# Gated mix of memory attention and a SiLU network on one core: q, k, v from scaled fp16 halves instead of float32r halves

## The chip, the cores and the metric

The kernel runs on one core of a Trainium2 chip. The metric is the device time of one execution in microseconds (us), from the kernel's start to its end. A core has TensorE (PE; its weight loads are listed as PEld), VectorE (DVE), ScalarE (ACT), GpSimd (POOL) and SyncE (SP), which here issues every DMA.

## The reference

x has 2048 rows of 448 features, 16 heads of 28 and 4 segments of 512 rows. Attention inside a segment adds the mask written below; between segments a linear memory carries over.

```python
q, k, v = x @ wq, x @ wk, x @ wv              # (16 heads, 4 segments, 512, 28)
phi = lambda t: jnp.where(t > 0, t + 1.0, jnp.exp(t))
g = sigmoid(beta)                              # one number a head
for s in range(4):
    mask = (ar[:, None] < ar[None, :]) * (-1e9)
    a_dot = softmax(qs @ ks.T * Dh ** -0.5 + mask) @ vs
    a_mem = (phi(qs) @ M) / (phi(qs) @ z + 1e-6)
    o = g * a_mem + (1.0 - g) * a_dot
    M, z = M + phi(ks).T @ vs, z + phi(ks).sum(rows)
a = o @ wo
b = silu(x @ w1) @ w2                          # 448 -> 1792 -> 448
gate = sigmoid((x * gate_w).sum(-1))
out = gate * a + (1 - gate) * b
```

## The kernel before, in words

Every float32 operand is kept as two halves, a high and a low part, and a product takes eleven matmuls: for each of three chunks of 128 features high·high, low·high and high·low, and two for the last 64 features, whose low part of x lies in the free half of the partitions (`passes`, line 368). `product` (L555) issues them and is also used by the feed-forward network and by the output projection, so L563 is the matmul line of all three.

There are two sorts of halves. For q, k, v before the change, `xquarter` (segment 0) and `xfeat` (segments 1 to 3) copy x into an xT tile as float32r (ACT, L779 and L795) and subtract to get the low part (DVE L783, L784; POOL L800, L802). `weight` does the same for wq, wk, wv (ACT L819, the subtraction at L822 on DVE or POOL). For the network, `halves` (L520) multiplies by a power of two first and stores fp16: ACT L523 for the high part, then `rest` (L512) for the low part, one DVE instruction (L515) or two POOL ones (L517, L518). `x16` (L531) loads x a second time, into rawf, and makes the fp16 tile xh of a segment with it; segment 0 during the projections, segments 1 to 3 inside the network.

The powers of two come from sizes. `size` (L380) reduces a tile to the largest absolute value of each partition (DVE L387). `scales(a, b)` (L398) turns columns a to b of these into scales: a reduction (L413), a transpose on PE (L417), four small DVE steps (L420 to L424), a broadcast on PE (L426), and two DVE steps that write the scale `up` and its inverse `top` (L430, L431). Index 0 to 3 is x of a segment, then WV, WQ, HQ (sixteen columns of w1 ride along in each block of wq and wk; HQ and HK scale their products), WK, HK, W1, W2, WO.

`project` (L699) is the first stage. For each block t of four heads in a segment (16 blocks) `proj` (L844) makes q and k in an "mm" bank of PSUM, evicts a high and a low fp16 half (ACT L853, DVE L855, both scaled by a column of `sqk`) and sends them to DRAM; where the memory needs it, it also makes phi: `pr` = relu(−t) from PSUM (ACT L869), `pe` = exp(−pr) (ACT L871), `ph` = max(t, 0) + pe (DVE L872). `vproj` (L892) makes v of 128 rows in an "sc" bank with the gate as a 449th column, and evicts it likewise (ACT L903, DVE L907, scaled by `sv`; ACT L905 takes the gate's exponential). `memory` and `retrieve` update and read the memory. `maxima` and `attention` are the masked attention, in the second stage, over which the network's matmuls are spread: `unit` (L1086) takes one segment's first matrix (L563 into mm), the SiLU (ACT L1098, DVE L1100, ACT L1102, DVE L1104), and the second matrix (L1121). The exponentials of attention are ACT L1224, the high half of their result ACT L1236, its low half POOL L1240, the product with v PE L1253. The last stage adds attention's output through wo.

The order on each engine is written when the program is built: `Sched` (L115) is a list scheduler. Tasks have an engine (or a choice of DVE and POOL: `either`, and `scaled` for two-pass work), a duration from a formula, dependencies, buffers that they take, and a priority; at each step the task that can start first goes next, and among equals the one of lower priority number. So the numbers at the head of the file (VC, QS, KS1, SS, OT1, XS, FIRST, WOT and others) move tasks against each other on every engine, and the engines then run that order strictly. Fifteen warm-up matmuls (L743) run at the very start.

Of the kernel before, what the change touches and what calls it, by code (L numbers as in the profile page):

```python
# [19 lines left out]
NG = 4  # L20
# [10 lines left out]
NEG = -1.0e30  # L31
NT = NSEG * NG
# [13 lines left out]
WOT = 59.67  # L46
# [8 lines left out]
SLACK = 0.88  # L55
LOP = 11.21
LATE = 0.08
FIRST = 120.0
WPRIO = 120.0
MAXO = 66.73  # L60
# [3 lines left out]
MP = 13.22  # L64
VF = 2.5
VA = 1.36
VS = 11.08
NV = 8
XS0 = 1.75
VC = -7.68  # L70
OT1 = 8.22
XS = 6.38
QS = -4.77
KS1 = 0.43
SS = 5.62
# [6 lines left out]
PRICE = 34.19  # L82
PVRUNS = [((1, 0), 1)]
PVP = 44.58
FLO = -16.6
FHI = 688.88
WOP = 89.36
SZ = 27.69
SZSTEP = 2.77
XPRIO = 87.67  # L90
WBP = -20.36
# [152 lines left out]
def infini_mix(ctx: ExitStack, tc: tile.TileContext, x, wq, wk, wv, wo, beta, w1, w2, out):  # L244
# [90 lines left out]
    WV, WQ, HQ, WK, HK, W1, W2, WO, NS = range(NSEG, NSEG + 9)  # L335
    cols, at = {}, 0
    for j, n in enumerate([4] * (NSEG + 5) + [FREE, FB, 4]):
        cols[j] = (at, at + n)
        at += n
# [11 lines left out]
    own2 = const.tile([128, 2], F32, name="own2")  # L351
    upw = const.tile([128, 3], F32, name="upw")
    sqk = const.tile([128, 2 * NSEG], F32, name="sqk")
# [4 lines left out]
    sv = const.tile([128, NSEG], F32, name="sv")  # L358
# [7 lines left out]
    X16 = {0: base.tile([128, 7, L], F16, name="xh0")}  # L366
# [11 lines left out]
    SIZE, SCALED, XH = {}, {}, {}  # L378
# [58 lines left out]
    LATER, GDONE, QREADY, KREADY, END1 = [], [], {}, {}, []  # L437

    def xi(s):
        return slice(NSEG - 1 - s, NSEG - s)  # L440

    def weigh(j, prio, *deps):

        def go():
            c = (j - WQ) // 2
            nc.vector.tensor_scalar(upw[:, 2:3], up[:, j:j + 1], own2[:, 0:1], None, op0=OP.mult)
            nc.vector.scalar_tensor_tensor(upw[:, c:c + 1], up[:, j + 1:j + 2], own2[:, 1:2], upw[:, 2:3], op0=OP.mult,
                                           op1=OP.add)
        return dve(350, go, SCALED[j], *deps, prio=prio)

    VREADY, PREADY, EREADY, OREADY = {}, {}, {}, {}

    def vscale(s, prio, *deps):
        VREADY[s] = dve(130, lambda: nc.vector.tensor_scalar(sv[:, s:s + 1], up[:, WV:WV + 1], up[:, xi(s)], 2.0 ** -26,
                                                             op0=OP.mult, op1=OP.mult), SCALED[NSEG - 1 - s], *deps, prio=prio)

    def qscale(s, prio, *deps):
        QREADY[s] = dve(130, lambda: nc.vector.tensor_scalar(sqk[:, s:s + 1], upw[:, 0:1], up[:, xi(s)], 2.0 ** -26,
                                                             op0=OP.mult, op1=OP.mult), SCALED[NSEG - 1 - s], *deps, prio=prio)

    def kscale(s, prio, *deps):

        def go():
            nc.vector.tensor_scalar(sqk[:, NSEG + s:NSEG + s + 1], upw[:, 1:2], up[:, xi(s)], 2.0 ** -26, op0=OP.mult,
                                    op1=OP.mult)
            if s < NSEG - 1:
                nc.vector.tensor_scalar(spk[:, s:s + 1], up[:, WK:WK + 1], up[:, xi(s)], 2.0 ** -25, op0=OP.mult, op1=OP.mult)
                nc.vector.tensor_scalar(spk[:, s:s + 1], spk[:, s:s + 1], UP, None, op0=OP.min)
        KREADY[s] = dve(400, go, QREADY[s], *deps, prio=prio)

    def others(s, prio, bds, own, t_own, t_gh):
# [13 lines left out]
        PREADY[s] = pool(600, spread_out, dve(260, go, VREADY[s], KREADY[s], prio=prio), t_own, t_gh, prio=prio)  # L485
# [45 lines left out]
    def x16(s, prio, *deps):  # L531

        ALL, END = slice(None), slice(REM, 128)
        XH[s] = []
        deps = [derive(s, SCALED[NSEG - 1 - s], prio), *deps]
        for c in range(4):
            r = Buf(RAW)
            d = dma(262e3, lambda c=c, r=r: start(r.v, x[s, :, c]), *deps, takes=[r], prio=prio + 0.01 * c)
            if s == 0:
                sl = slice(c * 128, (c + 1) * 128)  # L540
                hi = (ALL, slice(0, 4), sl)
                lo = [((ALL, slice(4, 7), sl), (ALL, slice(0, 3)), (ALL, slice(0, 3), sl)),
                      ((END, NC, sl), (END, NC), (END, NC, sl))]

                def src(r=r):
                    return r.v.rearrange("p (c n) -> p c n", c=4)
            else:
                hi = (ALL, c)
                lo = [((ALL, 4 + c), (ALL,), (ALL, c)) if c < NC else ((END, NC), (END,), (END, NC))]

                def src(r=r):
                    return r.v
            XH[s] += halves(NSEG - 1 - s, hi, lo, lambda: X16[s], src, L, d, prio + 0.01 * c, uses=[r])
# [37 lines left out]
    WA, WB = {}, {}  # L591
# [44 lines left out]
    XT, XDONE = {}, {}  # L636
# [62 lines left out]
    def project():  # L699
        es = ExitStack()  # L700
        wp = es.enter_context(tc.tile_pool(name="pw", bufs=1))
        XTR = cycle([wp.tile([128, 7, L], F32R, name=f"xT{i}") for i in range(2)])
        W = {n: wp.tile([128, 8, D + 2 if n == "v" else L], F32R, name=f"w{n}s") for n in "qkv"}
# [11 lines left out]
        ring("xraw", [128, L], F32, 6)  # L715
# [17 lines left out]
        def c1():  # L733
            for v in vtiles:
# [15 lines left out]
        LATER.append(dve(300, lambda: (nc.vector.tensor_reduce(own2[:, 0:1], ident[:, :GW], axis=AX.X, op=OP.max),  # L750
                                       nc.vector.tensor_reduce(own2[:, 1:2], ident[:, GW:], axis=AX.X, op=OP.max)), t_id, prio=-40))
# [8 lines left out]
        XR = {}  # L760

        def load_x(s, c, prio, *deps):
            b = Buf(R["xraw"])
            d = dma(262e3 if s else 170e3, lambda: start(b.v, x[s, :, c]), *deps, takes=[b], prio=prio)
            XR[s, c] = b, d
            if s:
                size(NSEG - 1 - s, lambda: b.v, L, d, uses=[b], prio=prio + XS)

        def xquarter(tb, prio):
            b, d = XR.pop((0, tb))  # L770
            if tb == 0:
                XT[0] = Buf(XTR)
                XDONE[0] = []
            xt = XT[0]
            sl = slice(tb * 128, (tb + 1) * 128)

            def view():
                return b.v.rearrange("p (c n) -> p c n", c=4)
            hi = act(L + 45, lambda: nc.scalar.activation(xt.v[:, 0:4, sl], view(), AF.Copy), d, *XDONE[0][:1],  # L779
                     takes=[] if tb else [xt], uses=[b, xt], prio=prio)  # L780

            def lo():
                nc.vector.tensor_sub(xt.v[:, 4:7, sl], view()[:, 0:3], raw(xt.v[:, 0:3, sl]))  # L783
                nc.vector.tensor_sub(xt.v[REM:128, NC, sl], view()[REM:128, NC], raw(xt.v[REM:128, NC, sl]))  # L784
            XC[0, tb] = [hi, dve(L + 64, lo, hi, uses=[b, xt], prio=prio)]
            XDONE[0] += XC[0, tb]
            size(NSEG - 1, lambda: b.v, L, XC[0, tb][1], uses=[b], prio=prio + XS0)

        def xfeat(s, c, prio):
            b, d = XR.pop((s, c))  # L790
            if c == 0:
                XT[s] = Buf(XTR)
                XDONE[s] = []
# [615 lines left out]
```

## Time and profile before

| what | value |
|---|---|
| median of the runs | 558.04 us (557.48 to 558.3, 3 runs) |
| span of the profiled execution, first to last instruction | 555.5 us |
| mean granted clock of TensorE | 0.997 |
| matmul records | 4007 |
| DMA moved | 85.87 MB, of which 52.60 MB read from and 26.09 MB written to HBM |
| last float32r matmul of q, k, v starts | 153.3 us |
| attention's last matmul with v starts | 466.6 us |

The profile gives the execution's span and no other time of its own; the runs lie 2.5 us above the span at the median, for what comes ahead of the first instruction and behind the last.

In a row of the groups or of the timeline stand the source line, the engine, the operation, the tile written and those read, the shapes and the count; in the groups behind a bar the busy time in us, the mean of one in ns, and the idle time of the engine just before them with what ended it. In the table by stage each engine has its busy time and its number of instructions. The chain of waits is followed back from the last instruction.

### The profile page before, as it was taken

To read this page: it belongs to the slowest core of one execution; us is meant where nothing else is said; L and a number is where in the kernel's file an instruction comes from. 1 tells how busy PE (TensorE), PEld (TensorE's weight loads), DVE (VectorE), ACT (ScalarE), POOL (GpSimd) and SP (SyncE) were. 2 spreads that over 40 slices of the span, in tenths; PEclk is the share of its full clock that TensorE was granted. 3 is DMA by queue.
4 is the path that set the end of the run, shared out by engine and by line. 5 is a ranking of instruction groups with operands and counts; after the bars stand their busy time and mean duration, and the time that the engine had idled before them with its cause. 6 is when DMAs were issued, how large, how long until landed. Compare 5 with 4: busy or idle time off the path is not lost.

```text
span 555.5 us, 11580 instructions
## 1 busy us (share of the span) xinstructions
PE 541.9 (98%) x4007; PEld 340.2 (61%) x4007; DVE 413.6 (74%) x1076; ACT 399.7 (72%) x695; POOL 365.2 (66%) x520
## 2 busy tenths in 40 slices
PE   8799999999999999999999999999999999999997
PEld 5588888888844555555656545565556555555544
DVE  6997998788789966789656888857997228745463
ACT  6467988876656878899778978878998897403140
POOL 5813648637320777999899979998999996212220
PEclk9899999999999999999999999999999999999999
DMA  8479888986775445423344235357302213689972
GB/s 293 153 241 217 229 220 242 224 213 188 216 211 163 130 136 176 122 74 79 108 118 127 68 88 155 108 139 180 90 19 70 69 50 94 226 208 222 251 183 83
DMA packets 91497, 85.87 MB, mean 155 GB/s; under 512 B 55432, under 2 KB 79112, under 8 KB 91440
## 3 DMA queue, kind: packets, MB, share of 16 engines
q1 hardware_dynamic: 91440, 85.15, 55.6%
q8 instruction: 31, 0.51, 0.4%
q14 instruction: 26, 0.21, 0.1%
HBM read 52.60 MB, written 26.09 MB: 142 GB/s over the span
## 4 chain that ended last, share of the span: by engine, by line
PE 84%; POOL 5%; DVE 4%; ACT 3%; DMA 2%; issue 2%; DVEq 0%; POOLq 0%; ACTq 0%
PE mm L563 32%; PE mm L1121 22%; PE sc L563 11%; PE sc L668 5%; PE sc L1219 5%; PE cc L1253 5%; POOL phl L1240 3%; DMA rawf<-in_x_dram 1%; ACT pf L1224 1%; PE cc L973 1%; ACT phl L1236 1%; DVE sizes L387 1%; PE cc L936 1%; DMA xraw<-in_x_dram 1%; PE cc L974 1%
## 5 line engine op out<-in xcount | busy, mean ns | idle before, releaser
L1240 POOL TENSOR_TENSOR phl<-pf,phl 128x384 f16<-128x384 f32 (+1 forms) x192 | 189.2, 1004 | 14.9 <-ACT phl L1236 14.8
L1121 PE MATMUL mm<-wb,ghl 128*128 128x448 f16 (+1 forms) x684 | 148.2, 349 | 0.0
L563 PE MATMUL mm<-xh,wa 128*128 128x512 f16 x572 | 140.3, 379 | 0.0
L1224 ACT ACTIVATE pf<-sc,es 128x512 f32<-128x512 f32 (+1 forms) x192 | 109.6, 620 | 15.7 <-PE sc L1219 12.6
L678 DVE CUSTOM_DVE_ANT_0 sc<-sc,mk 128x384 f32<-128x384 f32 (+1 forms) x192 | 104.6, 572 | 18.0 <-PE sc L668 16.6
L1121 PEld LDWEIGHTS <-ghl 128*128 128x128 f16 x684 | 64.7, 97 | 51.7 <-issue 1.0
L1236 ACT ACTIVATE phl<-pf 128x1280 f16<-128x1280 f32 x64 | 81.4, 1274 | 12.4 <-POOL pf L1230 12.3
L563 PEld LDWEIGHTS <-wa 128*128 128x128 f16 x572 | 53.6, 97 | 53.8 <-issue 0.3
L1219 PE MATMUL sc<-ring 86*128 86x512 f16 (+3 forms) x256 | 58.3, 299 | 2.2 <-ACT pf L1224 1.8
L668 PE MATMUL sc<-ring 84*128 84x128 f16 (+3 forms) x256 | 56.1, 299 | 0.5 <-ACT pf L1224 0.5
L1253 PEld LDWEIGHTS <-phl 128*128 128x128 f16 x1280 | 41.9, 96 | 8.8
L574 POOL TENSOR_TENSOR ol<-ol,ml 128x448 f32<-128x448 f32 x12 | 13.6, 1133 | 51.1 <-DMA ol<-o_scr 42.0
L563 PE MATMUL mm<-xT,wqs 128*128 128x512 f32 x176 | 47.2, 406 | 0.0
L563 PE MATMUL mm<-xT,wks 128*128 128x512 f32 x176 | 45.9, 400 | 0.0
L1098 ACT ACTIVATE th<-mm,ths 128x512 f32<-128x512 f32 x52 | 35.5, 689 | 13.3 <-PE mm L563 13.2
L1253 PE MATMUL cc<-vg,phl 128*128 128x29 f16 (+1 forms) x1280 | 43.6, 182 | 0.0
L1261 DVE TENSOR_REDUCE oraw<-cc 128x116 f32<-128x232 f32 x64 | 25.1, 393 | 23.3 <-PE cc L1253 23.1
L563 PE MATMUL sc<-wvs,xT 128*128 128x450 f32 x176 | 40.4, 373 | 1.0 <-DVE wvs L822 1.0
L1219 PEld LDWEIGHTS <-ring 86*128 86x128 f16 x256 | 24.5, 97 | 26.3 <-issue 3.5
L1227 POOL TENSOR_SCALAR_AFFINE_SELECT pf<-pf 128x128 f32<-128x128 f32 x64 | 20.9, 326 | 27.7 <-ACT pf L1224 25.3
L1104 DVE SCALAR_TENSOR_TENSOR ghl<-mm,ghl 128x512 f16<-128x512 f32 x52 | 35.1, 680 | 5.2 <-ACT ghl L1102 5.1
L1100 DVE SCALAR_TENSOR_TENSOR mm<-th,mm 128x512 f32<-128x512 f32 x52 | 35.4, 691 | 4.1 <-ACT th L1098 4.0
(162 smaller groups left out, 912.1 us busy)
## 6 DMA issues: line engine op xcount, KB each, us to landing
rawf<-in_w_dram SPq DMA_DIRECT2D x26, 256.0 KB
rawf<-in_w_dram SPq DMA_DIRECT2D x28, 224.0 KB
xraw<-in_x_dram SPq DMA_DIRECT2D x16, 256.0 KB
rawf<-in_x_dram SPq DMA_DIRECT2D x16, 256.0 KB
v_scr<-vt SPq DMA_DIRECT2D x16, 232.0 KB
vg<-v_scr SPq DMA_DIRECT2D x16, 232.0 KB
q_scr<-stg SPq DMA_DIRECT2D x16, 224.0 KB
k_scr<-stg SPq DMA_DIRECT2D x16, 224.0 KB
```

The lines of the kernel that those rows point to most:

```text
L563: nc.tensor.matmul(ps(), *p[i], start=(i == 0), stop=(i == n - 1))
L668: nc.tensor.matmul(ps.v[:, u:u + n], rg.v[:KS, 0, hh, i * 128:(i + 1) * 128], rg.v[:KS, 1, hh, :n], start=(i > 0), stop=(i > 0 or j == 3), ...
L678: nc.vector.tensor_tensor_reduce(r, r, MK[:, L - n:], 1.0, NEG, OP.add, OP.max, mx.v[:, hh, i:i + 1])
L1098: e1 = sact(L, lambda ps=ps, th=th: nc.scalar.activation(th.v, ps.v, AF.Tanh, scale=ths[:, s:s + 1]), m, takes=[th], uses=[ps], prio=p0)
L1100: e2 = dve(L, lambda ps=ps, th=th: nc.vector.scalar_tensor_tensor(ps.v, th.v, 1.0, ps.v, op0=OP.add, op1=OP.mult), e1, uses=[ps, th], prio=p0)
L1104: e4 = dve(L, lambda ps=ps, g=g: nc.vector.scalar_tensor_tensor(g.v[:, 1], ps.v, DOWN, g.v[:, 0], op0=OP.mult, op1=OP.subtract), e3, uses= ...
L1121: nc.tensor.matmul(ps.v[:, lo:hi], g.v[:, y, sl], w.v[:, z, lo:hi], start=(j == 0 and i == 0), stop=(j == len(fs) - 1 and i == 2))
L1219: nc.tensor.matmul(ps.v[:, e:e + w], rg.v[:KK, 1, hh, j * 128:(j + 1) * 128], rg.v[:KK, 0, hh, j * 128:], start=True, stop=True)
L1224: ex.append(sact(e, lambda b=b, ps=ps, pf=pf, e=e: nc.scalar.activation(pf.v[:, b, :e], ps.v[:, :e], AF.Exp, scale=es[:, s:s + 1]), m, *ex ...
L1236: hi = copy(1280, lambda hl=hl, flat=flat: nc.scalar.activation(hl.v[:, 0], flat(), AF.Copy), *mk, takes=[hl], uses=[pf], prio=p0 + 2)
L1240: low = pool(w - u, lambda hl=hl, flat=flat, u=u, w=w: nc.gpsimd.tensor_sub(hl.v[:, 1, u:w], flat()[:, u:w], hl.v[:, 0, u:w]), low, uses=[ ...
L1253: nc.tensor.matmul(p[:, i, :2 - z], hl.v[:, z, u:u + 128], vg.v[:, j, hh, :2 - z], start=(z == zs[0] and i == 0), stop=(z == zs[-1] and j ...
```

## The change

The float32r halves go. Segment x is loaded once, into xraw (eight buffers instead of six), in chunks of 128 features for segment 0 also (before, segment 0 came in quarters of its rows). Each chunk is measured, the segment's scale is made, and `halves` writes the fp16 tile xh, which q, k, v and later the network read; `x16`'s second loads from DRAM are gone, and xh of all four segments lies in the base pool. wv, wq and wk are measured, scaled and split by `halves` into fp16 tiles too, the head columns and the w1 columns of wq and wk separately, and the gate column has a scale of its own (WG). Every product of q, k and v therefore waits for the scales of x and of the weights. PSUM now holds scaled numbers, so the evictions use the constant FIT = 2^-26 instead of a column of `sqk` or `sv`, and wait for no scale; phi and the gate are scaled by `tqk` and `tg` instead. phi becomes relu(t) and exp(t), both read from PSUM, and min(exp, 1) + relu, from SBUF on DVE (one instruction) or POOL (two). The priorities are other numbers throughout.

```diff
-    X16 = {0: base.tile([128, 7, L], F16, name="xh0")}
+    X16 = {s: base.tile([128, 7, L], F16, name=f"xh{s}") for s in range(NSEG)}
...
+    def x16(s, c, prio):
+        r, d = XR.pop((s, c))
+        lo = [((ALL, 4 + c), (ALL,), (ALL, c)) if c < NC else ((END, NC), (END,), (END, NC))]
+        XH[s, c] = halves(NSEG - 1 - s, (ALL, c), lo, lambda: X16[s], lambda: r.v, L, d, prio, uses=[r])
...
-        XTR = cycle([wp.tile([128, 7, L], F32R, name=f"xT{i}") for i in range(2)])
-        W = {n: wp.tile([128, 8, D + 2 if n == "v" else L], F32R, name=f"w{n}s") for n in "qkv"}
+        W = {n: wp.tile([128, 8, D + 2 if n == "v" else L], F16, name=f"w{n}s") for n in "qkv"}
...
-        ring("xraw", [128, L], F32, 6)
+        ring("xraw", [128, L], F32, 8)
...
+        def whalves(name, prio, places):
+            for c, (b, _, v) in enumerate(places):
+                if name == "v":
+                    WS[name][c] = halves(WV, (ALL, c), [((ALL, 4 + c), (ALL,), (ALL, c))], dst, lambda v=v: v()[:, :D], D,
+                                         SCALED[WV], uses=[b], **k)
+                    continue
+                for j, sl, n in ((WQ if name == "q" else WK, slice(0, GW), D), (HQ if name == "q" else HK, slice(GW, 128), 64)):
+                    WS[name][c] += halves(j, (ALL, c, ALL, sl), [((ALL, 4 + c, ALL, sl), (ALL,), (ALL, c, ALL, sl))], dst, src, n,
+                                          SCALED[j], uses=[b], **k)
...
-            p = product(lambda: ps.v, lambda: passes(w, XT[s].v), L, prio,
-                        deps={c: WS[which][c] + (XC[s, c] if s else XDONE[0]) for c in range(NC + 1)}, takes=[ps],
-                        uses=[XT[s]])
+            p = product(lambda: ps.v, lambda: passes(w, X16[s]), L, prio,
+                        deps={c: WS[which][c] + XH[s, c] for c in range(NC + 1)}, takes=[ps], kind=half)
-            hi = sact(L, lambda: nc.scalar.activation(hl.v[:, 0], ps.v, AF.Copy, scale=sqk[:, k:k + 1]), p,
-                     (QREADY if which == "q" else KREADY)[s], takes=[hl], uses=[ps], prio=prio)
+            hi = act(L, lambda: nc.scalar.activation(hl.v[:, 0], ps.v, AF.Copy, scale=FIT), p, takes=[hl], uses=[ps], prio=prio)
...
-            tr = act(L, lambda: nc.scalar.activation(r.v, ps.v[:GW], AF.Relu, scale=-1.0), p, ...)
-            te = copy(L, lambda: nc.scalar.activation(e.v, r.v, AF.Exp, scale=-1.0), tr, ...)
-            tp = dve(L, lambda: nc.vector.scalar_tensor_tensor(ph.v, ps.v[:GW], 0.0, e.v, op0=OP.max, op1=OP.add), te, ...)
+            tr = sact(L, lambda: nc.scalar.activation(r.v, ps.v[:GW], AF.Relu, scale=tqk[:GW, k:k + 1]), p, ready, ...)
+            te = sact(L, lambda: nc.scalar.activation(e.v, ps.v[:GW], AF.Exp, scale=tqk[:GW, k:k + 1]), p, ready, ...)
+            def phi(eng):
+                if eng is nc.vector:
+                    eng.scalar_tensor_tensor(ph.v, e.v, 1.0, r.v, op0=OP.min, op1=OP.add)
+                else:
+                    eng.tensor_scalar(e.v, e.v, 1.0, None, op0=OP.min)
+                    eng.tensor_add(ph.v, e.v, r.v)
+            tp = scaled(L, phi, te, tr, takes=[ph], uses=[e, r], prio=prio)
...
         for tb in range(TB):
-            load_x(0, tb, -9 + 0.01 * tb + (0.5 if tb else 0))
+            load_x(0, tb, -9 + 0.01 * tb)
         weight("v", wv, -8.9, places[:4])
+        gate_size(-8.95, places)
+        scales(NSEG - 1, NSEG, -20)
         for tb in range(TB):
-            xquarter(tb, -9 + 0.01 * tb + (0.5 if tb else 0))
+            x16(0, tb, -8.8 + 0.01 * tb)
+        scales(WV, WG + 1, -20)
+        whalves("v", -8.6, places[:4])
...
-            if s + 1 < NSEG:
-                load_x(s + 1, g, max(o - 20, -4 + 0.1 * g), WLOAD[-1])
+            if s + 1 < NSEG and g == 0:
+                for c in range(NC + 1):
+                    load_x(s + 1, c, max(o - XLD, -4) + 0.1 * c, WLOAD[-1])
...
-        x16(0, XPRIO, SCALED[W1])
+        for s in range(NSEG):
+            DER[s] = derive(s, SCALED[W1], XPRIO)
...
-            if s not in XH:
-                x16(s, prio(0) - XLEAD, *list(t1.values())[:1])
```

More of the change, by code (lines that the diff above doesn't have):

```diff
@@ L54 @@
 HS = 0.14
[L55 to L56 removed]
+SLACK = 0.67
+LOP = 33.77
 LATE = 0.08
[L58 to L60 removed]
+FIRST = 104.18
+WPRIO = 134.65
+MAXO = 62.72
 FULL = 0.111
```

223 lines of the change are left out of this document (87 added, 136 removed).

## The prediction

> **What bounds the kernel now.** I read the busy shares of the page first, then its chain, then the table by stage.
>
> ```profile
> span 555.5 us, 11580 instructions
> PE 541.9 (98%) x4007; PEld 340.2 (61%) x4007; DVE 413.6 (74%) x1076; ACT 399.7 (72%) x695; POOL 365.2 (66%) x520
> PE 84%; POOL 5%; DVE 4%; ACT 3%; DMA 2%; issue 2%; DVEq 0%; POOLq 0%; ACTq 0%
> ```
> ```profile
> 0.00:156.00 156.00, 149.83 (x772) 122.01 (x773) 133.54 (x346) 114.30 (x242) 83.13 (x143) 0.99 0.80 220
> 30.00:156.00 126.00, 125.64 (x681) 105.32 (x680) 108.86 (x287) 96.48 (x208) 62.78 (x104) 1.00 0.83 219
> 60.00:100.00 40.00, 40.00 (x229) 33.61 (x228) 36.71 (x97) 35.42 (x79) 24.35 (x39) 1.00 0.87 220
> 156.00:470.00 314.00, 310.34 (x2801) 175.82 (x2800) 232.66 (x649) 263.97 (x418) 266.21 (x364) 1.00 0.39 111
> ```
> The columns are the stretch, its length, then PE, weight loads, DVE, ACT and POOL busy, the granted clock, DMA share and GB/s. TensorE is busy 98% of the span and holds 84% of the chain, so a microsecond of matmul slots removed is worth a microsecond, unless TensorE then waits. The projections end near 155 us. From 30 us on TensorE lacks 0.4 us there, but VectorE has little room: 36.71 of 40 us between 60 and 100. The first 30 us are different: TensorE waits there.
>
> **Part 1, matmul slots.** A listed matmul duration includes a drain that the next one overlaps, so I use spacings from the chain, and busy time of one tile's matmuls by stage.
>
> ```profile
> 106.74 2.26 PE sc L563 x11
> 109.00 2.50 PE mm L563 x11
> 112.35 2.57 PE mm L563 x11
> 155.07 13.83 PE mm L563 x64
> 481.08 8.32 PE sc L563 x44
> 30.00:156.00 126.00, 108.97 (x456) 82.95 (x454) 0.00 (x0) 4.87 (x8) 10.67 (x8) 1.00 0.83 219
> 30.00:156.00 126.00, 30.97 (x137) 24.88 (x135) 0.00 (x0) 0.00 (x0) 1.00 0.83 219
> ```
> The first three rows are float32r products: v 2.26/11 = 205 ns a matmul, q and k 2.50/11 = 227 ns, and 2.57 us where other work came in between. The next two are the fp16 products of the same shapes, of the network and of the output: 13.83/64 = 216 ns for 512 columns, 8.32/44 = 189 ns for 448. The last two give all matmuls reading xT after 30 us (456), and the 137 of v among them. The number of passes stays 11, of the same shape. Their 34 stretches each carry about 0.14 us of drain over the next instruction (estimate from 390 ns listed against 227 ns spacing), so 108.97 − 4.7 = 104.2 us. In fp16, 319 × 0.216 + 137 × 0.190 = 94.9 us. That is −9.3 us. The 72 before 30 us bring, at the same rate plus their many switches, about −2.5 us without the cold ones. Sum −11.8 us; pure spacing alone would give −6.7 us (32 products × 0.125, 16 × 0.17), the lower end.
>
> **Part 2, the start.** Now products start from plain float32r splits as soon as one chunk has landed; scales are wanted only at eviction. Afterwards x and wv must be measured, scaled and split first.
>
> ```profile
> 1.04 5.65 PE L743 MATMUL mm<-maskb 128*128 128x512 bf16 x15 [1.04 <-DVE ones L747]
> 5.20 0.63 ACT L779 ACTIVATE xT<-xraw 128x512 fp32r<-128x512 f32 x1 [3.13 <-DMA xraw<-in_x_dram]
> 6.40 0.50 PE L563 MATMUL sc<-wvs,xT 128*128 128x450 f32 x1
> 7.30 0.68 DVE L387 TENSOR_REDUCE sizes<-xraw 128x1 f32<-128x512 f32 x1
> 19.98 0.37 PE L417 MATMUL cc<-ident,most 128*2 128x128 f32 x1 [3.65 <-DVE most L413]
> 20.00 2.48 PE L563 MATMUL mm<-xT,wqs 128*128 128x512 f32 x5
> ```
> ```profile
> GB/s 0 0 68 149 107 268 334 353 383 381 388 404 385 388 410 410 396 404 336 377 404 150 0 0 0 76 150 167 147 134 290 401 311 82 0 0 0 332 302 120
> PE sc L563 <- DVE wvs L822: 1.0, 2, 0.5
> ```
> The GB/s row is the first 30 us in slices of 0.75 us. Summed, 1.05 MB (x, all of it now needed first and queued first) has moved at 6.3 us, and 2.0 MB (x and wv) at 8.7; the first chunk landed about 1.2 us after its bytes would say (5.2), so x is in at 7.3 and wv at 9.8. Measuring the last chunk of x takes 0.68: 8.0. A scale chain (reduce, transpose on TensorE, four small VectorE steps, broadcast, two steps) I put at 2.3 us: the four steps take 0.86, from 49.99 to 50.85 in the rows below, and I give the other five short ones 1.4 with their hand-overs: 10.3. The chain of wv, queued behind four reductions of some 0.6 us (450 columns of the 512), ends near 13.3, while ScalarE and VectorE split x. One wv chunk then takes about 0.65 on ScalarE (the 5.20 row's 0.63, now with a scale) and 0.68 on VectorE, and the gate column the rest: first product at 15.2 instead of 6.4, +8.8. Bounds: 12.5 if the wv chain is not held up, 18 if VectorE serves x splits first.
>
> ```profile
> 49.99 0.27 DVE L420 TENSOR_REDUCE few<-cc 1x1 f32<-1x128 f32 x1
> 50.65 0.20 DVE L424 TENSOR_SCALAR diag<-identb,few 1x1 bf16<-1x1 bf16 x1
> ```
> Against that, waits of before disappear: 3.65 on the q scales and 1.0 on wv halves, with 0.15 small ones, 4.8 us. Both have a cold clock: after the 3.65 us of idling, five matmuls take 2.48 us, about 427 ns each, a loss of some 1.3 us. Afterwards the idle stretch from the end of the warm-up (6.7 us) to 15.2 is longer, and its cold spell falls on v: 1.7. Then v (44 × 0.19 = 8.4 us) lasts to about 25.3, and q's halves need 8 reductions, a chain, 8 evictions and 8 subtractions, some 8 us of VectorE beside v's: nearly covered. k's follow behind q's four products (9.5 us), about as tightly, as do those of x for segment 1. I take 2 us of further idling, from 0 to 5. Sum: +8.8 − 4.8 + 0.4 + 2 = +6.4 us, between +2 and +12.
>
> **Part 3, loads in the network.** Sixteen second loads of x with their halves go.
>
> ```profile
> 216.93 3.83 DMA rawf<-in_x_dram
> 323.86 3.94 DMA rawf<-in_x_dram
> 223.08 0.63 PE L1219 MATMUL sc<-ring 86*128 86x384 f16 x3 [1.45 <-ACT pf L1224]
> 329.17 0.38 PE L664 MATMUL sc<-maskb,identb 128*128 128x512 bf16 x1 [0.90 <-ACT pf L1224]
> L523 ACT ACTIVATE xh<-rawf,up 128x512 f16<-128x512 f32 x12 | 8.8, 740 | 2.6 <-DMA rawf<-in_x_dram 2.6
> ```
> Twice ScalarE, which takes its work in order, stood at a split of x until the load landed; the exponentials behind it came late, and TensorE idled 1.45 and 0.90 us. That is −2.3 us. All idling of TensorE between 156 and 470 is 314.00 − 310.34 = 3.7 us, which is the most to be had; zero if the next late thing (the exponential and its subtraction on POOL) stalls the same place. The other loads and splits, and their issues on SP, lie beside TensorE work at a DMA share of 0.39: nothing. Only the 12 after 156 us count here; the 4 before, and all issue slots on SP, were covered too.
>
> **Part 4, evictions, phi and splits.**
>
> ```profile
> L855 DVE SCALAR_TENSOR_TENSOR stg<-mm,sqk,stg 128x512 f16<-128x512 f32 x32 | 23.6, 739 | 6.1 <-ACT stg L853 4.4 <-ACT pr L869 1.3 <-DMA h_scr<-stg 0.2
> L783 DVE TENSOR_TENSOR xT<-xraw,xT 128x384 fp32r<-128x384 f32 x4 | 3.2, 804 | 3.9 <-ACT xT L779 3.8
> L822 DVE TENSOR_TENSOR wvs<-raw,wvs 128x450 fp32r<-128x450 f32 x4 | 2.3, 620 | 0.0
> L515 DVE SCALAR_TENSOR_TENSOR wa<-rawf,up,wa 128x512 f16<-128x512 f32 x5 | 3.6, 744 | 0.0
> L515 DVE SCALAR_TENSOR_TENSOR xh<-rawf,up,xh 128x384 f16<-128x384 f32 x4 | 2.4, 592 | 1.6 <-ACT xh L523 1.6
> L800 POOL TENSOR_TENSOR xT<-xraw,xT 128x512 fp32r<-128x512 f32 x9 | 11.9, 1329 | 3.7 <-ACT xT L795 3.6
> L853 ACT ACTIVATE stg<-mm,sqk 128x512 f16<-128x512 f32 x32 | 21.6, 679 | 9.8 <-PE mm L563 7.3 <-DVE sqk L464 1.2 <-DVE sqk L458 1.0
> L869 ACT ACTIVATE pr<-mm 112x512 f32<-112x512 f32 x24 | 14.1, 589 | 1.2 <-PE mm L563 0.8 <-DVE stg L855 0.3
> L871 ACT ACTIVATE pe<-pr 112x512 f32<-112x512 f32 x24 | 15.2, 631 | 0.7
> ```
> ScalarE: a scale out of a tile costs 0.68 against 0.59 for a constant from PSUM. Evictions of q, k lose it (32 × −0.09); relu and exponential gain it (24 × 0.09 and 24 × 0.05); the splits of x cost 0.1 more each, those of q, k weights are twice as many; four splits of x leave this stage. Together about +1 us on an engine busy 114 of 156: nothing. The evictions no longer wait for q and k scales; relu and exponential wait instead, and the gate's exponential for its scale, with the next eviction queued behind it; by then the scales are old, except at 15 to 25 us (in Part 2). The PSUM bank of a product is read by three ScalarE steps and one VectorE step instead of a chain through phi, so it comes free sooner, worth nothing while TensorE never waits for one.
>
> VectorE: out go x's and wv's float32r remainders (about 8.6 us as L783, its half-height twin and L822 list them), the second split of x (2.4 and a half-height twin, about 3.9) and small scale steps (about 1.5): 14. In come up to 16 × 0.74 for x, 4 × 0.67 for wv, 8 × 0.9 for q and k: 21.8. Net +8 us at most, since each may go to POOL, which loses the remainders of L800 and of q's and k's weights, and pays about twice L800's 1.33 for one, in two passes. VectorE then has 133.5 to 141 us of work in a stage in which TensorE needs about 150. In the middle segments, already at 92%, I expect it to be late by some microseconds: its evictions hold the banks, and TensorE waits. Bounds 0 (all goes to POOL) and +8 (all stays, uncovered); I take +2.5, nearer to the row that shows TensorE full beside VectorE at 92%. The redrawn priorities I cost at nothing: beyond 30 us the trace has 4 us of TensorE idling to remove, counted above; they could lose 2.
>
> A rule to weigh is of the port between VectorE and POOL.
> ```profile
> L515 DVE SCALAR_TENSOR_TENSOR phh<-ph,spk,phh x12: 658/743/1236, 38.7 to 120.3; 112x512 f16<-112x512 f32 x12
> L872 DVE SCALAR_TENSOR_TENSOR ph<-mm,pe x24: 626/680/690, 30.0 to 150.6; 112x512 f32<-112x512 f32 x24
> ```
> These are minimum, median and maximum. phi's last step reads PSUM and never exceeds 690; the remainder of phi, with both inputs in SBUF, reaches 1236. The new phi has both inputs in SBUF. The Trainium skill ("SBUF — State Buffer", "Who interferes with whom") says that a VectorE instruction with two SBUF inputs contends with a GpSimd one that reads SBUF, and the later one is blocked outright. By that rule the two rows differ as they do; the trace agrees.
>
> **Sum.** −11.8 + 6.4 − 2.3 + 2.5 = −5.2 us on a span of 555.5. The runs' median is 558.04, 2.5 us above the span; I keep that: 552.8.
>
> **Rivals.** (a) The start costs less: first product at 13, no idling later, no lateness of VectorE: −11.8 + 2.2 − 2.3 = −11.9, 546 us. For it: POOL has 73 free microseconds in the stage. Against it: 5 to 30 us is one serial chain after another. (b) Slower: VectorE becomes the bound of the projections. With 141.4 us of work and its 22.5 us of present idling they end at 164 instead of 155: +9 − 2.3, about 564 us. It decides once TensorE waits more than 7.7 us for VectorE. For it: 36.71 of 40. Against it: POOL. (c) The port: each of 24 phi steps blocked as the phi remainders are (mean 781 against 658 minimum), 24 × 0.12 = +2.9 on VectorE, uncovered: 555.7. (d) Nothing: start lag and lateness eat the slots, 557 to 559; for it, every bound of Part 2 above +9.
>
> **How the numbers follow.** Within 0.2% (1.1 us) a measurement of this kernel can't tell from no change. Forecast, 549 to 555: 0.43. (a), 544 to 549: 0.20. (c), 555 to 556.9: 0.12. (d): 0.09. (b), 559.2 to 565: 0.16. Faster 0.75, same 0.09, slower 0.16. The range leaves out half of (a)'s and (b)'s far ends: 545.5 to 560.5; the forecast's own range is 549 to 555.
>
> **What would show it.** Right: q, k matmuls 216 ns apart and v 190; first product at 13 to 18 us, followed by a half clock; no x loads after 156 us, and no 1.45 us stall near 220; VectorE above 93% between 40 and 110 us. Wrong: TensorE idling more than 4 us between 30 and 150 us, stalls by exponentials that grow, or a first product after 18 us.

## The result, and the profile after

The kernel after runs in 553.07 us (551.65 to 553.42), the kernel before beside it in 558.17: a ratio of 0.9893, 95% interval 0.9863 to 0.9923. Faster by 1.1%; 552.8 was forecast. The profiled execution took 553.39 us with a span of 551.7, 3.8 less than before.

From the page, the span, the busy shares and the chain:
```profile
span 551.7 us, 11563 instructions
PE 534.8 (97%) x4009; PEld 294.7 (53%) x4009; DVE 409.3 (74%) x1074; ACT 391.8 (71%) x688; POOL 354.7 (64%) x519
PE 89%; DVE 4%; DMA 4%; ACT 1%; issue 1%; SPq 0%; DVEq 0%; ACTq 0%
```
The table by stage, columns as before (stretch, length, PE, weight loads, DVE, ACT, POOL, clock, DMA share, GB/s), with the first 30 us as a row of their own:
```profile
0.00:30.00 30.00, 17.26 (x59) 6.68 (x60) 22.66 (x72) 11.97 (x25) 5.25 (x30) 0.76 0.72 243
30.00:156.00 126.00, 126.00 (x716) 69.90 (x715) 116.06 (x293) 100.33 (x223) 71.14 (x111) 0.99 0.77 205
60.00:100.00 40.00, 40.00 (x238) 22.88 (x237) 38.99 (x100) 35.51 (x83) 19.57 (x30) 1.00 0.92 230
156.00:470.00 314.00, 313.55 (x2821) 177.57 (x2820) 226.30 (x635) 260.79 (x411) 263.45 (x366) 1.00 0.38 106
```
Behind 30 us TensorE is full: 126.00 of 126 and 313.55 of 314 us, where before it lacked 0.4 and 3.7. VectorE stands at 38.99 of 40 between 60 and 100 and holds nobody up. The price is in the first row: 17.26 us of TensorE in 30 us. The same row of the kernel before:
```profile
0.00:30.00 30.00, 24.20 (x93) 16.68 (x94) 24.68 (x61) 17.82 (x34) 20.35 (x39) 0.94 0.66 225
```
So 12.7 us of idling against 5.8, and a mean clock of 0.76 against 0.94. Two rows of the chain show the new spacing, 2.10/11 = 191 ns for v and 2.37/11 = 215 ns for q and k:
```profile
115.66 2.10 PE sc L540 x11
122.09 2.37 PE mm L540 x11
```
The start on TensorE, from the timeline (start, duration, what; in brackets the idle time and what ended it):
```profile
9.32 0.37 PE L418 MATMUL cc<-ident,most 128*1 128x128 f32 x1 [2.86 <-DVE most L414]
11.66 0.16 PE L427 MATMUL cc<-diag,oneb 1*128 1x1 bf16 x1 [1.97 <-DVE diag L425]
12.98 0.37 PE L418 MATMUL cc<-ident,most 128*2 128x128 f32 x1 [1.16 <-DVE most L414]
14.56 0.16 PE L427 MATMUL cc<-diag,oneb 2*128 2x2 bf16 x1 [1.21 <-DVE diag L425]
16.85 0.53 PE L540 MATMUL sc<-wvs,xh 128*128 128x450 f16 x1 [2.13 <-ACT wvs L516]
18.31 5.68 PE L540 MATMUL sc<-wvs,xh 128*128 128x450 f16 x19 [0.93 <-DVE wvs L508]
...
27.21 0.27 PE L418 MATMUL cc<-ident,most 128*2 128x128 f32 x1 [0.43 <-DVE most L414]
28.21 0.39 PE L540 MATMUL mm<-xh,wqs 128*128 128x512 f16 x1 [0.73 <-ACT wqs L516]
28.89 2.21 PE L540 MATMUL mm<-xh,wqs 128*128 128x512 f16 x5 [0.29 <-DVE wqs L508]
```
Two scale chains in a row, x's and wv's, stand ahead of the first product. Then 19 matmuls take 5.68 us where 3.6 would do, and five of q's take 2.21 where 1.1 would: in this execution there are two spells at half clock, not one. Stretches cut at their edges show them (the clock is the last number but two):
```profile
8.50:22.30 13.80, 5.58 (x16) 2.17 (x17) 13.53 (x42) 5.20 (x10) 0.28 (x1) 0.51 0.97 342
22.30:29.00 6.70, 5.25 (x27) 2.32 (x26) 5.09 (x19) 4.49 (x12) 0.00 (x0) 1.00 0.33 111
29.00:32.50 3.50, 3.50 (x10) 1.09 (x9) 3.40 (x10) 3.21 (x11) 3.21 (x6) 0.51 0.49 155
```

### The profile page after: what moved, and what is told of

The parts are those of the page before. It is cut to its first block, busy times and chain, and to the rows that moved or that the text cites. A ratio compares the mean times of both kernels' runs of the same rounds, so it can differ in the third digit from the quotient of the medians.

```text
span 551.7 us, 11563 instructions
## 1 busy us (share of the span) xinstructions
PE 534.8 (97%) x4009; PEld 294.7 (53%) x4009; DVE 409.3 (74%) x1074; ACT 391.8 (71%) x688; POOL 354.7 (64%) x519
## 4 chain that ended last, share of the span: by engine, by line
PE 89%; DVE 4%; DMA 4%; ACT 1%; issue 1%; SPq 0%; DVEq 0%; ACTq 0%
PE mm L540 31%; PE mm L1086 23%; PE sc L540 12%; PE sc L1182 6%; PE sc L644 6%; PE cc L1216 6%; DMA rawf<-in_w_dram 2%; PE cc L932 1%; DMA xraw<-in_x_dram 1%; PE cc L895 1%; DVE sizes L388 1%; DVE sc L654 1%; DMA v_scr<-vt 1%; PE sc L640 1%; PE cc L933 0%
## 5 line engine op out<-in xcount | busy, mean ns | idle before, releaser
L644 PE MATMUL sc<-ring 84*128 84x128 f16 (+3 forms) x256 | 58.2, 299 | 0.1
L540 PE MATMUL mm<-xh,wqs 128*128 128x512 f16 x176 | 44.5, 390 | 1.0 <-ACT wqs L516 0.7
L540 PE MATMUL sc<-wvs,xh 128*128 128x450 f16 x176 | 39.9, 368 | 3.1 <-ACT wvs L516 2.1
L540 PE MATMUL mm<-xh,wks 128*128 128x512 f16 x176 | 42.1, 380 | 0.0
L1067 ACT ACTIVATE ghl<-mm 128x512 f16<-128x512 f32 x52 | 30.9, 604 | 6.5 <-DVE mm L1065 6.4
```

Of the source, the lines that this page charges most:

```text
L540: nc.tensor.matmul(ps(), *p[i], start=(i == 0), stop=(i == n - 1))
L644: nc.tensor.matmul(ps.v[:, u:u + n], rg.v[:KS, 0, hh, i * 128:(i + 1) * 128], rg.v[:KS, 1, hh, :n], start=(i > 0), stop=(i > 0 or j == 3), ...
```

## The experiments

In all, twelve more kernels ran. Each ratio is to runs of the kernel before on the same chip; those had medians of 558.1 to 558.7. Only x_first ran the work of the kernel after on a chip of the experiments, so other differences from 553.07 us are uncertain by some tenths. Idling of TensorE "in all" is counted from its first matmul to its last.

### Do the shorter slots alone bring their microseconds?

f16_plain: the kernel before with fp16 tiles for xT and W, no scaling, the order of all tasks as it was.
```diff
-        XTR = cycle([wp.tile([128, 7, L], F32R, name=f"xT{i}") for i in range(2)])
+        XTR = cycle([wp.tile([128, 7, L], F16, name=f"xT{i}") for i in range(2)])
```
(and the same for W)

> The kernel before, with xT, wq, wk and wv stored as fp16 instead of float32r and nothing else touched: no scaling, the same order on every engine, the second loads of x still there. The low halves are so small that part of their last bits is lost. Theory (a matmul slot is what the change gains): TensorE takes about 9.3 us less from 30 us on; of the 2.5 us before that most is lost, since v then only waits longer for the q scales. 547 to 549 us. Rival (VectorE, which does the same work as before in less time, makes TensorE wait): the gain stays under 6 us, 552 us or more, with TensorE idling over 3 us between 30 and 150 us.

555.44 us, ratio 0.9945 (0.9928 to 0.9961): 3 us and not some 10. The first 30 us kept the full clock, and yet TensorE idled 4.67 us between 30 and 156. Its stage row:
```profile
30.00:156.00 126.00, 121.33 (x688) 66.50 (x687) 110.32 (x295) 96.66 (x208) 62.37 (x106) 1.00 0.84 222
```
The largest of its waits in that stretch (total, times, longest):
```profile
PE cc L974 <- POOL phq L878: 3.8, 4, 1.6
```
TensorE now reaches the retrieval before GpSimd has made phi's remainder: the order was drawn for slower products. The rival's figures came true, through GpSimd and not through VectorE. A slot that gets shorter is banked only if what comes next on the engine is ready.

### What are the redrawn priorities worth?

old_prios: the kernel after with the numbers of the kernel before at the head of the file (VC, QS, KS1, SS, MP, VS, XS and the others; the new ones, XH0 and XLD, stay).

> The kernel after the change, with the priorities (the numbers at the head of the file) of the kernel before; everything else of the change stays. As the prediction has it, priorities are worth nothing: within 1.5 us of the kernel after, 552 to 555. The rival, from the run with x and weights in fp16 alone, where TensorE idled 4.7 us in a fitting order lost: an order drawn for slower products idles TensorE by 3 us or more between 30 and 156 us, and the time is 556 or more.

569.08 us, ratio 1.0207 (1.0183 to 1.0232), 16 us behind the kernel after, and slower than before. The rival held, and by far. Its stages:
```profile
0.00:30.00 30.00, 16.92 (x67) 7.04 (x67) 22.75 (x72) 11.07 (x25) 4.75 (x28) 0.83 0.78 248
30.00:156.00 126.00, 116.05 (x610) 62.64 (x611) 104.61 (x277) 93.67 (x206) 62.95 (x95) 0.92 0.70 185
156.00:470.00 314.00, 313.29 (x2782) 178.54 (x2781) 225.07 (x634) 257.20 (x408) 252.71 (x358) 1.00 0.37 106
```
The two largest of its waits between 30 and 156 us:
```profile
PE cc L427 <- DVE diag L425: 2.6, 4, 0.9
PE cc L895 <- DVE top L432: 2.3, 2, 1.7
```
The start and the network are nearly as in the kernel after. The loss lies between 30 and 156 us: 9.95 us of idling and a clock of 0.92. Half of the idling, 4.9 us, is TensorE standing at a scale chain that is not done; the rest is spread over waits for phi's remainders, for halves of x and wq, and for v and the memory, none longer than about 1.2 us. VectorE, at 104.61, has time to spare there.

old_scales: the same, but with the four numbers that place the scale chains as the kernel after has them.
```diff
-VC = -7.68
+VC = -4.07
...
-SS = 5.62
+SS = -13.76
```


> The kernel after with the priorities of the kernel before, which came out at 569 us, but with the four that place the scale chains (VC, QS, KS1, SS) as the kernel after has them. Theory: the 16 us came mainly from scale chains that TensorE reaches before they are done (waits of 6.8 us on diag, 2.3 on top, and cold clock behind them), so at least half comes back: 553 to 561. Rival: the loss lies in the whole order (memory, retrieval, second half of x, v), and these four alone bring back 3 us or less: 566 or more.

562.32 us, ratio 1.0074 (1.0057 to 1.009): 6.8 of the 16 us come back, between what the two sides expected. TensorE has 125.49 of 126 us in the stage again, but idles 3.9 in the network and 16.6 in all, 4.4 more than in the kernel after. So the chains' places are a large part, and not all, of what the order is worth.

early_xh: the kernel before, with the second loads of x in the network moved far ahead by their priority.
```diff
-XLEAD = 146.82
+XLEAD = 400.0
```


> The kernel before, with one number changed: the second loads of x for segments 1 to 3 get a priority 253 units lower (earlier). Theory (the network's stalls came from ScalarE standing at a late load of x): TensorE's 3.7 us of idling between 156 and 470 us shrinks to about 1, 555 to 556 us. Rival (the idling comes from attention's own order and the load only happened to be last): no change, 557.5 to 558.5 us.

573.88 us, ratio 1.0276 (1.0263 to 1.0289). A miss, and no test of the loads: the planner (the list scheduler that writes the order) drew all engines anew behind the first moved task, and between 156 and 470 us TensorE came to 303.44 of 314 us, with three more spells of half clock.

### What is sharing the halves worth in the network?

ffn_reload: the kernel after, with x of segments 1 to 3 loaded and split a second time ahead of its network, as before.
```diff
+            if i == 0 and s:
+                reload(s, prio(0) - XLEAD, *list(t1.values())[:1])
```


> The changed kernel, with one part undone: segments 1 to 3 of x are loaded and split a second time inside the network, with the priority that the kernel before used. Theory (sharing x with the network is worth what the stalls cost, 2.3 to 3.6 us): 555 to 557 us, with TensorE idling 2 us or more between 156 and 470 us. Rival (another order hides the loads, so sharing is worth nothing): within 0.7 us of 553.1.

557.01 us, ratio 0.998 (0.9957 to 1.0003): some 4 us given back, as expected, though its runs spread from 555.02 to 564.2. Its largest waits behind 156 us:
```profile
PE mm L540 <- DVE ghl L1069: 1.9, 1, 1.9
PE sc L1195 <- DVE mx L654: 1.0, 1, 1.0
```
Stalls return, in other places and behind VectorE: 1.2 us of idling up to 470 us, under the 2 us expected, and 1.9 us of the first wait just behind 470. That they are those of the extra splits, and not of the order that they shift, this run does not separate.

### How near is VectorE to being the bound?

dve_extra: the kernel after with eight more reductions of 0.68 us on VectorE behind products of q, 5.4 us in all.
```diff
+            if which == "q" and 4 <= t < 12:
+                END1.append(dve(L, lambda: nc.vector.tensor_reduce(junk, MK, axis=AX.X, op=OP.max), p, *MKS, prio=prio))
```


> The changed kernel, with eight extra VectorE reductions of a constant 128x512 tile (about 0.68 us each, 5.4 us in all), one behind each q product of segments 1 and 2; their results are not used. Theory (VectorE, busy 97% between 60 and 100 us, stands right at the edge of making TensorE wait): 3 to 5 us longer, 556 to 558 us, with as much idling of TensorE between 50 and 120 us. Rival (there is slack: banks and later stretches absorb it): under 1 us longer, 554 us or less.

556.94 us, ratio 0.9968 (0.9956 to 0.998), 3.9 us more. TensorE idles 1.2 us at once behind an eviction (L811 is L807 there). The stage row, and the wait:
```profile
60.00:100.00 40.00, 38.78 (x226) 21.87 (x225) 39.26 (x102) 34.38 (x80) 26.24 (x33) 1.00 0.90 223
```
```profile
PE mm L540 <- DVE stg L811: 1.2, 1, 1.2
```
That fits a stage at the edge: in the kernel after VectorE costs nothing, and some microseconds more of it do. But the planner drew the order anew here too. Of TensorE's idling only 1.4 us came between 30 and 156 us, and 1.4 more in the network, where none of the eight stands; so how much of the 3.9 is VectorE's and how much the order's stays open.

### phi, and the port

phi_only: the kernel before, with the new phi alone (both functions from PSUM, then min and add), as a task that may go to VectorE or GpSimd.

> The kernel before, with phi alone changed: relu and exponential both from PSUM, then min and add from SBUF on VectorE or GpSimd. As the prediction has it, nothing on the path: within 1.1 us of the kernel before, the new phi on VectorE at 0.62 us when undisturbed and up to 1.2 when GpSimd reads SBUF. The rival (c) of the prediction: 24 steps longer by 0.12 us each, uncovered, 2.9 us slower, with TensorE waiting between 60 and 110 us.

567.94 us, ratio 1.0171 (1.015 to 1.0192). Its phi on VectorE never took over 0.96 us, so that the port does not explain it; the order had changed on every engine, TensorE idled 13.4 us in all instead of 8.8, and its mean clock fell to 0.983. So it was repeated with the order held.

phi_frozen: the new phi in the places of the old one; the order on every engine is that of before. pr has two halves for it, used in turn.
```diff
-            te = copy(L, lambda: nc.scalar.activation(e.v, r.v, AF.Exp, scale=-1.0), tr, ...)
-            tp = dve(L, lambda: nc.vector.scalar_tensor_tensor(ph.v, ps.v[:GW], 0.0, e.v, op0=OP.max, op1=OP.add), te, ...)
+            te = copy(L, lambda: nc.scalar.activation(e.v, ps.v[:GW], AF.Exp), tr, ...)
+            tp = dve(L, lambda: nc.vector.scalar_tensor_tensor(ph.v, e.v, 1.0, r.v[:, z], op0=OP.min, op1=OP.add), te, ...)
```


> The kernel before with the new phi (relu and exponential from PSUM, min and add from SBUF on VectorE), the order of all instructions on every engine left as it was. Theory, after the run with phi alone came out 9 us slower in an order of its own: the loss there was the order's, and phi by itself is worth nothing, within 1.1 us of the kernel before. Rival (c) of the prediction, the port between VectorE and GpSimd: 24 steps longer by 0.12 us each, 2.9 us slower, with TensorE idling more between 60 and 110 us.

565.58 us, ratio 1.0128 (1.011 to 1.0146): 7.5 us slower. The theory fell; rival (c) of the prediction is real, and larger than it was priced. phi in this kernel (shortest, median, longest):
```profile
L875 DVE SCALAR_TENSOR_TENSOR ph<-pe,pr x24: 626/683/1733, 29.7 to 158.7; 112x512 f32<-112x512 f32 x24
```
Its stage row, where TensorE loses 3.9 us:
```profile
60.00:100.00 40.00, 36.09 (x203) 28.77 (x202) 35.87 (x87) 30.85 (x71) 26.13 (x37) 1.00 0.77 199
```
One of the collisions, in the timeline of GpSimd and of VectorE:
```profile
116.34 1.29 POOL L881 TENSOR_TENSOR phq<-ph,phq 112x512 fp32r<-112x512 f32 x1 [0.38 <-ACT phq L879]
116.44 1.73 DVE L875 SCALAR_TENSOR_TENSOR ph<-pe,pr 112x512 f32<-112x512 f32 x1
```
And the same pair in the kernel before, with phi from PSUM:
```profile
101.17 1.29 POOL L878 TENSOR_TENSOR phq<-ph,phq 112x512 fp32r<-112x512 f32 x1
101.30 0.68 DVE L872 SCALAR_TENSOR_TENSOR ph<-mm,pe 112x512 f32<-112x512 f32 x1
```
A phi that starts 0.1 us behind a GpSimd subtraction ends 0.5 us after that one has ended; with one input in PSUM it runs beside it in 0.68. Ten of the 24 took over 0.75 us (none before), and each of the ten began while a GpSimd instruction was running. The mean rose from 676 to 920 ns, 24 × 0.244 = 5.9 us on VectorE, and TensorE's largest wait is again at the retrieval, for phi's remainder on GpSimd. Part of the 7.5 us may be another's: ScalarE's relu waited 4.6 us for phi to free pr, which before only the exponential read. The rule of the Trainium skill ("SBUF — State Buffer", "Who interferes with whom") that the shared port is an exclusive lock agrees with both pairs of rows.

In the kernel after the same phi does little harm:
```profile
L829 DVE SCALAR_TENSOR_TENSOR ph<-pe,pr x22: 616/682/1432, 45.6 to 150.4; 112x512 f32<-112x512 f32 x22
```
Three of 22 took over 0.75 us; the mean in the groups is 722 ns. There phi is a task of the kind `scaled`, and for such a task the planner keeps VectorE and GpSimd apart:
```python
        if eng == "POOL" or eng == "DVE" and t.port:
            s = max(s, self.port["DVE" if eng == "POOL" else "POOL"] + LOCK)
```

### The start

x_first: the kernel after, meant to hold wq's loads until x had landed.
```diff
-                WLOAD.append(dma(170e3, lambda c=c, v=v: start(v(), src[:, c]), ...
+                WLOAD.append(dma(170e3, lambda c=c, v=v: start(v(), src[:, c]), *after, ...
```


> The kernel after, with the loads of wq held on SP until the four chunks of x's first segment have landed; the order on every engine is the same. Theory: x's last chunk landed at 8.25 us and not at 7.3 because loads of weights in flight share the DMA engines with it; then it lands about 1 us earlier, and the first product of v starts near 16 us and not 16.85; the time falls by 0.5 to 1 us if q's halves follow, by nothing if wq then comes too late. Rival: the landing is set by the number of descriptors or the latency of the chunk itself, and x lands at 8.2 again.

553.01 us, ratio 0.9901 (0.9885 to 0.9918), but it held nothing: a dependency in the plan puts a load later in the order and gives it no wait, and the loads came out as they had been:
```profile
4.96 3.66 SPq L324 DMA_DIRECT2D raw<-in_wq_dram  x4
```
So it tells nothing of its theory, and is a second measurement of the kernel after, 0.06 us from the first.

hold_w: the kernel after, where a copy of a few columns on ScalarE, from x's last chunk into the weights' buffer, makes all loads of weights wait.
```diff
+        held = act(32, lambda: nc.scalar.activation(raw0.v[:, 0, :32], xl.v[:, :32], AF.Copy), dl, takes=[raw0], ...)
+        weight("v", wv, -8.9, places[:4], held)
```


> The kernel after, where a small ScalarE copy from x's last chunk into the buffer of the weights makes the loads of wv, wq and wk wait until all of x's first segment has landed (in the run x_first nothing was held: its first load of wq was issued at 4.96 us). Theory: x's last chunk lands at about 7.3 us, as predicted, since 0.54 of the 1.59 MB that moved up to its landing at 8.25 were weights. Rival: it lands at 8.2 again. The time is no test: wv comes some 3 us later, 553 to 557 us.

561.69 us in one run; the time says nothing of the landing, and lay above the 553 to 557 that were expected. The copy that waits for x's last chunk in its timeline:
```profile
6.62 0.23 ACT L961 ACTIVATE raw<-xraw 128x32 f32<-128x32 f32 x1 [4.55 <-DMA xraw<-in_x_dram]
```
The reduction that waits for the same chunk in the kernel after:
```profile
8.25 0.69 DVE L388 TENSOR_REDUCE sizes<-xraw 128x1 f32<-128x512 f32 x1 [1.06 <-DMA xraw<-in_x_dram]
```
x alone is in at 6.6 us, earlier than the theory's 7.3, and by 8.25 with weights in flight. In six of the other kernels that start with these loads the last reduction began between 8.0 and 8.6; in one, warm_merged below, x was in by 6.6 with the weights in flight as well. So it is likely, and by one run of hold_w not shown, that sharing delays x, by up to 2 us and not in each execution.

warm_all: the kernel after with 40 filler matmuls on a tile of zeros between the steps of the scale chains, in the gaps where TensorE waits; all other work in its order.
```diff
+        def keep(n, *deps):
+            prev[:] = [sch.add("PE", 0.001, lambda: [nc.tensor.matmul(
+                wb.v, wz, wz[:, None, :].to_broadcast([128, 4, 128]), start=True, stop=True) for _ in range(n)], ...
+        FILL.update({"go": keep, (NSEG - 1, 0): 12, (NSEG - 1, 1): 8, (NSEG - 1, 2): 4, (WV, 1): 4, (WV, 2): 9, (WK, 1): 3})
```


> The kernel after, with filler matmuls on a tile of zeros between the steps of the scale chains, so that TensorE stays busy up to the first products; the order of all other work is the same. Theory: the two half-clock spells at 8.6 to 22.2 and 29.0 to 32.5 us cost about 4 us (v's first 12 matmuls 2.2, q's first 9 matmuls 1.9), and go: 2 to 4 us less than the kernel after. Rival: after v the start is bound by VectorE's scaling of wq, so that q's first product stays near 28 us; then only q's cold matmuls are won, 1.9 us or less.

549.01 us, ratio 0.9838 (0.982 to 0.9855): 4.0 us less than the kernel after (x_first, on the same chip). The theory held; the rival's 28 us did not. The first 30 us, and two rows of the timeline:
```profile
0.00:30.00 30.00, 25.26 (x111) 10.45 (x112) 24.22 (x76) 13.85 (x32) 6.63 (x33) 1.00 0.77 258
```
```profile
18.25 3.80 PE L547 MATMUL sc<-wvs,xh 128*128 128x450 f16 x19 [1.11 <-DVE wvs L515]
26.42 0.38 PE L547 MATMUL mm<-xh,wqs 128*128 128x512 f16 x1
```
The 19 matmuls of v take 3.80 us instead of 5.68 from the same start, q begins at 26.42 instead of 28.21 and at full clock. This version beats both kernels.

warm_merged: warm_all with one scale chain for x's first segment and wv, 26 fillers ahead of it, the splits of x and wv in turn, and QS at −8.0 instead of −15.23.
```diff
-        scales(NSEG - 1, NSEG, -20)
+        scales(NSEG - 1, WG + 1, -20)
```


> The kernel after with the filler matmuls, and one scale chain for x's first segment and wv together instead of two, one behind the other; the splits of x and wv alternate. Theory: the first product of v starts at about 15 us instead of 16.8, and 1 to 2 us are won over the kernel with fillers alone: 547 to 548. Rival: the first product waits for the remainders on VectorE anyway, so that the start ends as late as with two chains, and the new order elsewhere decides: 549 to 553.

554.92 us, ratio 0.9943 (0.9927 to 0.996). Too many fillers: the chain's sizes were reduced at 11.05 us, and the transpose came behind them at 12.84. The first product still began at 16.32 and q's at 23.92, 2.5 us ahead of warm_all, but TensorE then came to 122.84 of 126 us between 30 and 156 in the order that was drawn anew. The late transpose, and the largest wait of that stage:
```profile
12.84 0.27 PE L423 MATMUL cc<-ident,most 128*3 128x128 f32 x1
```
```profile
PE cc L951 <- POOL phq L856: 1.9, 1, 1.9
```
A better start was lost again in a worse order; the rival's mechanism, beyond its range.

## Why the prediction came out right, point by point

The total was 0.3 us off, and that closeness is luck. The start cost 4.9 us more than forecast, the network brought 0.9 more and VectorE's lateness did not come, so that sizes cancelled; and one step, the price of the order, was wrong as it was put.

| term | forecast | measured |
|---|---|---|
| slots, warm | −11.8 | −11.9 |
| start | +6.4 | +11.3 |
| stalls in the network | −2.3 | −3.2 |
| VectorE's lateness | +2.5 | 0 |
| idling of 0.4 us from 30 to 156 us | counted in no term | −0.4 |
| sum | −5.2 | −4.2, span −3.8 |

The table is made of two profiles, whose spans differ by 3.8 us; the medians differ by 5.1. A run lies some 1.7 us above its own span (553.39 and 551.7 here). So the profiled execution of before, with its span of 555.5, was some 0.8 us faster than its kernel's median (an estimate from that 1.7), and the one after 0.3 slower.

**Slots: right, its size in part by luck.** I summed TensorE's times from each matmul's start to the next one's, without its idling, from both traces: q, k and v go from 122.97 to 111.38 us, the retrieval's matmuls from 10.73 to 13.17, together −9.15. In it is what the cold clock costs, 1.3 us before and 4.1 after (some 12 of v's matmuls at 375 ns instead of 190, some nine of q's at 427 instead of 216). Without it: −11.9. But q, k and v alone bring −14.4, more than the −11.8 of the sum, and the retrieval takes back 2.4 that no term named. The retrieval is the surprise: its first matmul, still float32r, takes 212 ns instead of 160. It now follows fp16 products; that an exposed switch moved there from q's products is my reading, not tested.

**Start: right in kind, mis-sized.** The idling grew by 6.9 us (12.7 against 5.8), the cold clock by 2.8, and the small matmuls of the scale chains by 1.6 (start-to-start, 2.7 against 1.1 us). The failing terms: x landed at 8.25 and not at 7.3, for the estimate gave x all the bytes that moved first, and at 8.25 us 1.63 MB had moved for 1.05 MB of x; the first product came at 16.85, not 15.2; and the second half-clock spell, on q, was not in the sum. The cold spell on v, put at 1.7, was 2.2, and the one on q 1.9 more. With the fillers, which leave all other work in its order, those 4 us are gone.

**Network: right, a little larger.** The last idle time went with the second loads: 3.66 to 0.45 us, near the 3.7 that was named as the most; putting the loads back costs some 4 us, with the order changed by them.

**VectorE: the lateness of 2.5 did not come.** Its work up to 156 us rose from 133.54 to 138.72 us (22.66 and 116.06), within the bounds. The row says 97.5% busy between 60 and 100 us. Between 40 and 110, where above 93% was named, it is busy 66.88 of 70 us, and TensorE does not wait. Eight reductions more cost 3.9 us, in another order. Two things were missing in the count: evictions with a constant are cheaper on VectorE too (below), and only two of 24 phi steps went to GpSimd.

**Priorities: the step that failed.** "The redrawn priorities I cost at nothing" holds only against a TensorE that is full already. Part 1 banked its slots by assuming that it stays full; with the priorities of before it does not, and the change loses 10.5 us against the kernel before instead of gaining 5. The order was worth 16 us to this change, and the forecast of the total held because the redrawn order delivers what Part 1 took for given. No run gave the kernel before a new set of numbers, so what such a search would bring without the change stays open.

**Rival (c)** was priced at +2.9 and did not happen, yet the mechanism exists, and where phi was put in the old places the kernel lost 7.5 us, the larger part of it probably by this (5.9 us more on VectorE). That it stayed small in the kernel after I put down to the planner's rule on tasks that may go to both engines, which I had not weighed; no run takes the rule away. Rival (a) fell because the start was dearer than forecast, and not cheaper; (b) because VectorE did not become the bound; (d), that the start eats the slots, came near: in the two profiles the start took 11.3 of the slots' 11.9 us, and what is left of the gain is mostly the network's.

## What to carry to other kernels

When an instruction gets faster on an engine that runs a fixed order, ask for each next instruction whether its inputs will be ready that much earlier; the order is part of the change, and a test of one part in an order drawn anew tests the order. Hold the order still to test a part, as phi_frozen did. And where the bound engine must wait at the start, give it something to do: 40 filler matmuls were worth 4 us.

## What the runs showed of the hardware

- A spell of half clock needs no long pause, but short pauses do not always bring one. In the profile of the kernel after TensorE idled 0.43, 0.73 and 0.29 us between 26.7 and 29.0 us (row 22.30:29.00: 5.25 of 6.70 busy), and the clock was 0.51 from 29.0 to 32.5. The profiles of dve_extra and ffn_reload have the same pieces and the same spell. In x_first, with the same pieces (0.43, 0.72, 0.29), the five matmuls of q behind them ran at full clock, in 1.25 us instead of 2.21:
```profile
29.41 1.25 PE L540 MATMUL mm<-xh,wqs 128*128 128x512 f16 x5 [0.29 <-DVE wqs L508]
```
  The Trainium skill ("TensorE: Matmul & The Clock Gate", "HAM oscillation — how this bites in real kernels") warns of gaps above about 3.4 us; here much shorter ones, close together, sufficed in three profiles of four, and the measurement decides. What separates the fourth is not shown.
- A scale that is a constant is cheaper than one read from a tile on both engines, for the same shapes: the eviction's high half 594 ns instead of 679 on ScalarE, which was foreseen, and the low half 679 instead of 739 on VectorE, which was not:
```profile
L807 DVE SCALAR_TENSOR_TENSOR stg<-mm,stg 128x512 f16<-128x512 f32 x32 | 21.6, 679 | 3.1 <-ACT stg L806 1.7 <-ACT pe L824 1.4
L806 ACT ACTIVATE stg<-mm 128x512 f16<-128x512 f32 x32 | 19.0, 594 | 7.8 <-PE mm L540 7.7
```
- Loads queued first do not always land first at full rate: x's four loads are issued from 0.79 to 2.61 us, the weights' behind them, and at 8.25 us, when the last of x was in, 1.63 MB had moved for 1.05 MB of x. In warm_merged, with the same issues, x was in by 6.6.
